# V's second last half in two transfers of 1 MB, and half of its P.V ahead of the merge of head 14

## The chip, the cores and the metric

The kernel runs on one core of one Trainium2 chip. Times are device microseconds (us) of one execution. A shorter time is better. The engines are named as in the profile: PE (matrix multiply), PEld (its weight loads), DVE (vector), ACT (activation), POOL, and SP, whose queue issues the large transfers. "Granted clock" is the share of its full clock that the chip lets PE have. All executions quoted were fast, that is, none was more than 1.5% above the fastest of its kernel.

## The reference

One query row attends to 8192 keys, in each of 16 heads of width 256, in bf16.

```
B, H, Sq, Sk, D = 1, 16, 1, 8192, 256
# q: [B,H,Sq,D], k and v: [B,H,Sk,D], all bf16
scores = einsum("bhqd,bhkd->bhqk", q, k) * D ** -0.5
p = softmax(scores, axis=-1)
return einsum("bhqk,bhkd->bhqd", p, v)
```

K and V together are 134.2 MB, and each of their elements is used once. The kernel can't take less time than their transfer.

## The kernel before

Each head's K and each head's V come in two halves of 2 MB. A half has 32 columns, and a column is a 128x256 piece of bf16. The halves are numbered 0 to 31, so head 14 has 28 and 29, and head 15 has 30 and 31. The first half of K and the last half of V already came in pieces:

```python
HALF = 32
V_SLOTS = 2 * UNROLL          # 4 buffers for halves of V
FIRST_CUT = (4, 4, 8, 16)
LAST_CUT = (16, 8, 4, 4)
# ...
        def cuts(kind, n):
            if kind == "k" and n == 0:
                return FIRST_CUT
            if kind == "v" and n == NIT - 1:
                return LAST_CUT
            return (HALF,)
```

All K and V transfers are issued in a fixed order on SP's queue. Each piece has a semaphore, and a transfer waits only until its buffer is free:

```python
        for kind, h, x in items:
            # ... n: number of the half, slot = n % slots
            if n >= slots:
                waits = [f"{kind}free{n - slots}"] + ([f"ktfree{n - slots}"] if kind == "k" else [])
            cs = cuts(kind, n)
            at = 0
            for i, wd in enumerate(cs):
                if kind == "k":
                    s = sem_l[slot] if i == 0 else s_first[i - 1]
                else:
                    s = sem_l[slot] if i == len(cs) - 1 else s_last[i]
                used[id(s)] = used.get(id(s), 0) + 16
                plan.op("sp", ..., f"{kind}{n}.{i}", waits, dma=(s, used[id(s)]))   # (cut)
                at += wd
```

P.V of a half, `pv`, multiplies the softmax weights (`E`) with the columns of V and adds up in the accumulator `acc`. It runs on PE and waits column by column for the piece that holds the column. Head 15 takes one column of V at a time, the other heads take two. For those, `merge` adds the two partial rows that this leaves, with weights from DVE:

```python
        def pv(n, c0=0, c1=HALF):
            # ... head h, buffer slot, accumulator a
            step = 1 if h == H - 1 else 2
            for c in range(c0, c1, step):
                pe(lambda e, c=c, col=col: e.matmul(
                        a[0:step, 0 : step * D],
                        lhsT=E[:, col : col + step],
                        rhs=Vb[slot][:, c * D : (c + step) * D],
                        start=(x == 0 and c == 0), stop=(x == 1 and c == HALF - step)),
                    f"vfree{n}" if c == HALF - step else None,
                    [f"e{h}", first_free] + landed("v", n, c, c + step))

        def merge(h):
            act(...)                 # copies acc[s][0:2, :] to ac[s], waits for vfree{2*h+1}
            for i in range(2):
                pe(...)              # acc[s][0:1, 0:D] += w2[:, i].T @ ac[s][:, i*D:(i+1)*D]
```

This is the end of the program on PE, after its loop over the heads. The loop's last pass ends with P.V of half 27 and the merge of head 13.

```python
        n = 2 * (H - 2)
        pv(n)                            # half 28
        softmax(H - 1)
        pv(n + 1, 0, HALF // 2)          # half 29
        softmax2(H - 1)
        pv(n + 1, HALF // 2, HALF)
        lmm(H - 1)                       # row sums of head 15
        n += 2
        pv(n, 0, HALF // 4)              # half 30: 8 columns
        merge(H - 2)
        final(H - 2)
        # ... output of heads 0 to 14, from ACT's queue
        pv(n, HALF // 4, HALF)           # half 30: 24 columns
        pv(n + 1)                        # half 31
        final(H - 1)
        # ... output of head 15
```

## Time and profile before

| | before |
|---|---|
| median of the first three runs, us | 327.12 (326.97 to 327.27) |
| profiled execution, us | 327.36, span 325.6 |
| landings of V's half 29, half 30 and the last piece of half 31, us | 310.27, 315.18, 320.15 |
| PE's last matmul ends, us | 323.51 |

From the page of the kernel before: busy time by engine, then lines of the forty slices of the span. A digit is tenths of a slice of 8.14 us, PEclk is the granted clock in tenths.

```profile
PE 238.7 (73%) x1746; PEld 112.4 (35%) x1746; DVE 281.4 (86%) x1624; ACT 100.8 (31%) x200; POOL 0.2 (0%) x4
...
PEclk9999999969899898979598989779689877898999
DMA  7999999999999999999999999999999999999990
...
q1 hardware_dynamic: 10080, 134.22, 97.4%
```

The DMA engines are busy for 90% or more of all slices except the first and the last, and queue q1, with K and V, keeps them busy for 97.4% of the span. This kernel waits for bytes. A change that moves no bytes can gain only at the end, where the bytes have come and work is left.

The timeline of PE in that end, kernel before. The columns are start, us from the first start to the last end, engine and line, operation, output and inputs, count. In brackets stand the idle time just ahead and what ended it. L610 is P.V, L632 the merge, L589 the row sums.

```profile
300.51 3.62 PE L610 MATMUL acc<-Vb,E 128*2 128x512 bf16 x16 [0.84 <-DMA Vb<-in_v_dram]
304.80 1.02 PE L632 MATMUL acc<-ac,w 2*1 2x256 f32 x4 [0.68 <-ACT ac L625]
305.75 3.61 PE L610 MATMUL acc<-Vb,E 128*2 128x512 bf16 x16
...
310.31 1.89 PE L610 MATMUL acc<-Vb,E 128*2 128x512 bf16 x8 [0.73 <-DMA Vb<-in_v_dram]
...
314.16 0.19 PE L589 MATMUL misc<-ones_col,lsum 128*2 128x1 f32 x2
315.32 1.03 PE L610 MATMUL acc<-Vb,E 128*1 128x256 bf16 x8 [0.96 <-DMA Vb<-in_v_dram]
316.28 1.02 PE L632 MATMUL acc<-ac,w 2*1 2x256 f32 x4
317.23 6.27 PE L610 MATMUL acc<-Vb,E 128*1 128x256 bf16 x56
```

The first three lines are P.V of half 27, the merge of head 13, and P.V of half 28. PE waits 0.73 us for half 29 and 0.96 us for half 30, and after 315.32 it waits for nothing. At that time half 31 is still arriving, but always ahead of PE.

The chain of waits of the same kernel, at its end, in order of time (start, length, what). Here and below, pieces of it named "issue", of 0.14 us or less, are left out.

```profile
296.77 18.41 DMA Vb<-in_v_dram
315.32 1.03 PE acc L610 x8
316.35 0.95 PE acc L632 x4
317.30 6.22 PE acc L610 x56
323.54 0.47 ACT o L654
```

The transfer in this chain is half 30, issued at 296.77 when P.V of half 26 freed its buffer. From its landing on, everything is work of PE and then one copy on ACT.

### The profile page before, as it was taken

What the parts mean: (1) busy time and instruction counts of PE and PEld (TensorE: products, weight loads), DVE (VectorE), ACT (ScalarE), POOL (GpSimd) and SP (SyncE); (2) the same over time, 40 slices, a digit from 0 to 9 for tenths busy, and PEclk for the clock granted to TensorE, in tenths of its full rate; (3) what the DMA queues carried; (4) which work ended last, traced back from release to release, by engine and by line L of the source; (5) the groups of instructions that cost most, each with busy time, mean ns of one, the idle gap of its engine ahead of it and who ended that gap; (6) DMA issues with size and microseconds to landing.
All of it is one profiled execution on the core that took longest, in us unless ns stands there. A gap on an engine that the chain in (4) does not pass through costs nothing.

```text
span 325.6 us, 5646 instructions
## 1 busy us (share of the span) xinstructions
PE 238.7 (73%) x1746; PEld 112.4 (35%) x1746; DVE 281.4 (86%) x1624; ACT 100.8 (31%) x200; POOL 0.2 (0%) x4
## 2 busy tenths in 40 slices
PE   1554328788787868787878866887786788777977
PEld 0333223343333333333334333332333324333335
DVE  3799999999999999999999998888988888988400
ACT  2362321332424242333133242222324213242110
POOL 0000000000000000000000000000000000000000
PEclk9999999969899898979598989779689877898999
DMA  7999999999999999999999999999999999999990
GB/s 256 426 437 425 426 429 425 431 429 425 428 433 427 425 431 433 421 431 431 427 427 431 429 425 433 431 421 432 433 423 427 428 433 423 431 431 425 431 387 19
DMA packets 10126, 134.35 MB, mean 413 GB/s; under 512 B 1138, under 2 KB 1155, under 8 KB 1924
## 3 DMA queue, kind: packets, MB, share of 16 engines
q1 hardware_dynamic: 10080, 134.22, 97.4%
q8 instruction: 4, 0.07, 0.1%
q14 instruction: 6, 0.05, 0.0%
q10 hardware_dynamic: 36, 0.02, 0.0%
HBM read 134.23 MB, written 0.01 MB: 412 GB/s over the span
## 4 chain that ended last, share of the span: by engine, by line
DVE 52%; DMA 34%; PE 6%; issue 5%; ACT 1%; DVEq 1%; SPq 0%
DVE prod L362 48%; DMA Kb<-in_k_dram 18%; DMA Vb<-in_v_dram 16%; PE acc L610 5%; DVE S L362 2%; DVE w L341 1%; PE acc L632 1%; DVE g L331 1%; ACT KT L504 0%; DVE colf L285 0%; DVE recip L339 0%; DVEq L144 0%; ACT ac L625 0%; DVE m L381 0%; PE tp L495 0%
## 5 line engine op out<-in xcount | busy, mean ns | idle before, releaser
L362 DVE CUSTOM_DVE_ANT_0 prod<-Kb,qbc 128x256 bf16<-128x256 bf16 x768 | 269.3, 411 | 21.5 <-DMA Kb<-in_k_dram 12.5
L610 PE MATMUL acc<-Vb,E 128*2 128x512 bf16 (+1 forms) x544 | 148.2, 437 | 7.1 <-DMA Vb<-in_v_dram 7.0
L504 ACT ACTIVATE KT<-tp 128x1024 bf16<-128x1024 bf16 x64 | 62.0, 1021 | 115.1 <-PE tp L495 115.1
L610 PEld LDWEIGHTS acc<-Vb,E 128*2 128x2 bf16 (+1 forms) x544 | 49.8, 95 | 91.6 <-issue 49.0
L362 DVE DVE_READ_ACCUMULATOR2_ANT S<- 128x1 f32 x768 | 56.7, 74 | 0.0
L495 PE MATMUL tp<-identb,Kb 128*128 128x128 bf16 x512 | 38.2, 234 | 5.0 <-DMA Kb<-in_k_dram 5.0
L521 PE MATMUL spe<-qcur,KT 128*128 128x1 bf16 x512 | 21.6, 165 | 23.3 <-ACT KT L504 23.2
L495 PEld LDWEIGHTS tp<-identb,Kb 128*128 128x128 bf16 x512 | 32.3, 105 | 15.8 <-issue 14.9
L521 PEld LDWEIGHTS spe<-qcur,KT 128*128 128x128 bf16 x512 | 16.8, 98 | 28.9 <-ACT KT L504 28.7
L625 ACT ACTIVATE ac<-acc 2x512 f32<-2x512 f32 x15 | 8.8, 587 | 58.0 <-PE acc L610 58.0
L632 PE MATMUL acc<-ac,w 2*1 2x256 f32 x60 | 15.3, 373 | 9.5 <-ACT ac L625 9.5
L560 PE MATMUL misc<-g,ones_row 1*128 1x1 f32 x32 | 6.8, 280 | 17.3 <-DVE g L331 17.3
L549 PE MATMUL misc<-ident,m 128*1 128x128 f32 x34 | 7.1, 293 | 14.7 <-DVE m L381 14.7
L560 PEld LDWEIGHTS misc<-g,ones_row 1*128 1x128 f32 x32 | 5.5, 213 | 20.4 <-DVE g L331 19.9
L647 ACT ACTIVATE o<-acc 1x256 bf16<-1x256 f32 x15 | 5.6, 373 | 17.9 <-PE acc L632 17.9
L632 PEld LDWEIGHTS acc<-ac,w 2*1 2x1 f32 x60 | 3.5, 77 | 20.9 <-ACT ac L625 16.6
L549 PEld LDWEIGHTS misc<-ident,m 128*1 128x1 f32 x34 | 1.5, 81 | 21.5 <-DVE m L381 15.3
L331 DVE TENSOR_REDUCE g<-misc 1x1 f32<-1x128 f32 x17 | 4.7, 274 | 5.0 <-PE misc L549 5.0
L567 ACT ACTIVATE negb<-misc 128x1 f32<-128x1 f32 x16 | 2.8, 174 | 13.6 <-PE misc L560 13.6
L339 DVE RECIPROCAL recip<-misc 2x1 f32<-2x1 f32 x17 | 2.6, 151 | 4.5 <-PE misc L589 4.5
L589 PE MATMUL misc<-ones_col,lsum 128*2 128x1 f32 x34 | 3.2, 164 | 3.9 <-ACT E L574 3.1
L574 ACT ACTIVATE E<-S,negb 128x64 bf16<-128x64 f32 x16 | 5.6, 348 | 0.5
(34 smaller groups left out, 39.6 us busy)
## 6 DMA issues: line engine op xcount, KB each, us to landing
Kb<-in_k_dram SPq DMA_DIRECT2D x31, 2048.0 KB, 23.4
Vb<-in_v_dram SPq DMA_DIRECT2D x31, 2048.0 KB, 28.2
Kb<-in_k_dram SPq DMA_DIRECT2D x1, 1024.0 KB, 7.8
Vb<-in_v_dram SPq DMA_DIRECT2D x1, 1024.0 KB, 13.5
Kb<-in_k_dram SPq DMA_DIRECT2D x2, 256.0 KB, 3.0
Kb<-in_k_dram SPq DMA_DIRECT2D x1, 512.0 KB, 4.5
Vb<-in_v_dram SPq DMA_DIRECT2D x1, 512.0 KB, 14.3
Vb<-in_v_dram SPq DMA_DIRECT2D x2, 256.0 KB, 14.6
```

The costliest lines, as they stand in the source:

```text
L331: lambda e: e.tensor_reduce(g[0:1, s : s + 1], misc[s][0:1, MT0 : MT0 + P], AX.X, ALU.max),
L362: lambda e, slot=slot, c=c, col=col, h=h, r=(ttr - 1) % PROD: e.tensor_tensor_reduce(out=prod[:, r * D : (r + 1) * D], in0=Kb[slot][:, c * ...
L495: lambda e, c=c, hf=hf, i=(b * NH + hf) * P, view=view: e.transpose(view[:, i : i + P], Kb[slot][:, c * D + hf * P : c * D + (hf + 1) * P] ...
L504: lambda e, gn=gn, view=view: e.activation(out=KT[gn % KT_SLOTS][:, :], in_=view[:, 0 : GROUP * D], func=ACT.Copy),
L521: lambda e, b=b, hf=hf, oc=oc, gn=gn: e.matmul(spe[sl(h)][:, oc : oc + 1], lhsT=KT[gn % KT_SLOTS][:, (b * NH + hf) * P : (b * NH + hf + 1) ...
L549: lambda e: e.matmul(misc[s][0:1, MT0 : MT0 + P], lhsT=m[:, s : s + 1], rhs=ident[:, :], start=True, stop=True),
L560: lambda e: e.matmul(misc[s][:, BC0 : BC0 + 1], lhsT=ones_row[0:1, :], rhs=g[0:1, s : s + 1], start=True, stop=True),
L574: lambda e: e.activation(out=E[:, s * J : (s + 1) * J], in_=S[:, s * J : (s + 1) * J], func=ACT.Exp, bias=negb[:, h : h + 1], scale=SCALE, ...
L610: lambda e, c=c, col=col: e.matmul(a[0:step, 0 : step * D], lhsT=E[:, col : col + step], rhs=Vb[slot][:, c * D : (c + step) * D], start=(x ...
L625: lambda e: e.activation(out=ac[s][:, :], in_=acc[s][0:2, :], func=ACT.Copy),
L632: lambda e, i=i: e.matmul(acc[s][0:1, 0:D], lhsT=w2[0:2, 2 * s + i : 2 * s + i + 1], rhs=ac[s][0:2, i * D : (i + 1) * D], start=(i == 0), ...
L647: lambda e: e.activation(out=o[0:1, h * D : (h + 1) * D], in_=acc[s][0:1, 0:D], func=ACT.Copy),
```

## The change

The intent: the columns of half 30 that PE needs first should not wait for the columns that it needs last. The half comes in two transfers of 1 MB, and the whole of the first is used before the merge of head 14.

```diff
+BEFORE_CUT = (16, 16)
...
-        s_last = [sem(f"s_l{i}") for i in range(len(LAST_CUT) - 1)]
+        s_last = [sem(f"s_l{i}") for i in range(len(LAST_CUT) + len(BEFORE_CUT) - 2)]
...
                 return LAST_CUT
+            if kind == "v" and n == NIT - 2:
+                return BEFORE_CUT
             return (HALF,)
...
-                    s = sem_l[slot] if i == len(cs) - 1 else s_last[i]
+                    s = sem_l[slot] if i == len(cs) - 1 else s_last[i + (len(LAST_CUT) - 1) * (n == NIT - 2)]
...
-        pv(n, 0, HALF // 4)
+        pv(n, 0, HALF // 2)
         merge(H - 2)
         final(H - 2)
...
-        pv(n, HALF // 4, HALF)
+        pv(n, HALF // 2, HALF)
         pv(n + 1)
```

## The prediction

> **What bounds the kernel.** The transfers. The page gives the DMA engines 97% of the span at 413 GB/s; the forty slices show them full until about 317 us of 325.6. PE is busy 73%, DVE 86%. Only the tail can gain from this change: everything before waits for bytes whose number and order stay.
>
> **The tail, from the timeline of PE and the landings in the trace.** V's last halves land 4.9 us apart: number 29 at 310.27, 30 (the changed one) at 315.18, and 31, already in four pieces, at 317.67, 318.88, 319.51 and 320.15 us. PE starts P.V of 29 at 310.31 and works without a gap until the row-sum matmul of head 15 ends at 314.35. Then it is idle 0.96 us, released by the DMA of Vb at 315.32 (the chain of waits goes through that 18.41 us transfer too). From there PE never idles: 8 columns of head 15, merge of head 14 (first matmul 316.28), 56 columns from 317.23 to 323.50. A column costs (323.50 - 317.23)/56 = 0.112 us, the merge holds PE 0.95 us. A copy on ACT (0.47) and the output's DMA end the run. The last V byte lands 3.3 us before PE ends, so this stretch is PE-bound.
>
> **What the change does.**
> 1. Half 30 comes as two transfers of 1 MB, in order on one queue, so the first should be complete half of 4.91 us before the second: 315.18 - 2.45 = 312.7 us (an estimate from these landings). PE is free only at 314.35: its 0.96 us wait goes whole, with 1.6 us to spare. The Trainium skill ("DMA: Bandwidth & Descriptors", Why a DMA increments its semaphore by 16) says that only the full 16 means that all has landed; the trace agrees: for half 30, fifteen increments are in by 313.86, the last at 315.18. I put the same lag into the 312.7.
> 2. Sixteen instead of eight columns before the merge: 8 x 0.112 = 0.9 us moves ahead of it, nothing is added. The merge's inputs are ready either way: the ACT copy ends at 314.95, DVE's weights at 314.81; eight columns from 314.35 would end at about 315.25. I expect the move alone to be worth about 0.
> 3. One more issue on SP's queue, 0.33 to 0.43 us, after that at 296.77; the next issue waits until 304.16 for a buffer, so it is hidden. Half 31 took 4.97 us in four pieces against 4.91 in one: cutting should cost under 0.1 us, against over 1 us of slack.
>
> **New tail.** PE starts head 15 at 314.35: 16 columns to 316.15, merge to 317.1, 48 columns to 322.5. Needs: second half of 30 at 317.1 (landed 315.2); 31's pieces at 318.9, 320.7, 321.6, 322.0 (landed 317.7, 318.9, 319.5, 320.2). No new wait. Gain 0.96 to 1.0 us, all on the critical path.
>
> **Predicted time** 327.12 - 0.97 = 326.15 us, range 325.8 to 326.55. Faster by over 2%: 0.01; within 2%: 0.98; slower: 0.01.
>
> **Right or wrong in the profile.** The 0.96 us idle before head 15's first columns is gone; the first 1 MB lands near 312.7; merge begins near 316.1; PE ends near 322.5, with no wait on 31's pieces; the last landing stays near 320.2; before 310 us nothing differs.
>
> **What would make it wrong.** The first piece landing after 314.35; smaller pieces delaying half 31 by over 1 us; a half-clock window (3.4 us, granted 0.5 elsewhere in the trace; the tail from 295.9 us had 1.0) falling on the tail, costing up to 1.7 us.

## The result, and the profile after

| | before | after |
|---|---|---|
| median, us (six runs each) | 327.28 (326.97 to 328.11) | 326.19 (325.47 to 327.01) |
| profiled execution, us | 327.36, span 325.6 | 326.87, span 325.1 |
| V's landings: 29, first of 30, all of 30, all of 31, us | 310.27, none, 315.18, 320.15 | 310.09, 312.58, 315.06, 320.07 |
| PE's last matmul ends, us | 323.51 | 323.03 |

The ratio is 0.9965, with a 95% interval of 0.9944 to 0.9985. A ratio here is the mean time of one kernel's fast runs over that of the other's in the same rounds, so it isn't quite the ratio of the medians. The change is a gain clear of noise, about 1.1 us by the medians, and within 2%.

The lines of the page after that answer to those of before:

```profile
PE 237.1 (73%) x1746; PEld 112.2 (35%) x1746; DVE 281.3 (87%) x1624; ACT 101.0 (31%) x200; POOL 0.2 (0%) x4
...
PEclk9999999979898996979797989877898697798799
DMA  7999999999999999999999999999999999999991
...
q1 hardware_dynamic: 10224, 134.22, 97.6%
```

The queue has 144 packets more: 128 rows are cut in two, and there are 16 more semaphore increments. The bytes and the load of the engines are the same. One thing differs that the change doesn't touch: in PEclk, the third digit from the end (the slice from 300.7 to 308.8 us) is a 7, and it was a 9 before. The trace's clock records have a window of 3.41 us at half clock from 301.49 us, and before has no such window after 295.88.

The timeline of PE in the tail, kernel after. The line numbers have moved by three (P.V is now L613, the merge L635).

```profile
300.34 5.30 PE L613 MATMUL acc<-Vb,E 128*2 128x512 bf16 x16 [0.85 <-DMA Vb<-in_v_dram]
306.32 1.02 PE L635 MATMUL acc<-ac,w 2*1 2x256 f32 x4 [0.68 <-ACT ac L628]
307.27 3.61 PE L613 MATMUL acc<-Vb,E 128*2 128x512 bf16 x16
...
310.94 1.89 PE L613 MATMUL acc<-Vb,E 128*2 128x512 bf16 x8
...
314.79 0.19 PE L592 MATMUL misc<-ones_col,lsum 128*2 128x1 f32 x2
314.84 1.91 PE L613 MATMUL acc<-Vb,E 128*1 128x256 bf16 x16
316.68 1.02 PE L635 MATMUL acc<-ac,w 2*1 2x256 f32 x4
317.63 5.40 PE L613 MATMUL acc<-Vb,E 128*1 128x256 bf16 x48
```

The wait for half 30 is gone, as intended. The wait for half 29 is gone too, which the change can't have done. P.V of half 27 took 5.30 us instead of 3.62, because the half-clock window fell on it, so PE came to half 29 late. That is why this pair of profiles differs by 0.5 us where the medians differ by 1.1.

The end of the chain of waits, kernel after:

```profile
265.49 34.81 DMA Vb<-in_v_dram
300.34 5.32 PE acc L613 x16
305.68 0.60 ACT ac L628
306.32 1.02 PE acc L635 x4
307.34 3.54 PE acc L613 x16
...
317.70 5.35 PE acc L613 x48
```

Before, the last transfer in the chain was half 30, and PE's share began at 315. After, the last transfer is half 27, and the chain stays on PE (with one copy on ACT) from 300 us on. This is the second effect of the change: the tail is no longer held by a transfer near its end, so it now depends on how fast PE ran in the 15 us before.

### A reading without the start's noise

Executions differ by up to 1.1 us in when V lands, whatever the kernel. I therefore measured each profiled execution's tail from its own landings. The last column is the time of that execution minus V's last landing, and the window is any half-clock window starting between 295 and 315 us.

| kernel (profiled execution) | half-clock window | head 15 starts after half 29 landed, us | PE ends after V's last landing, us | time minus V's last landing, us |
|---|---|---|---|---|
| before | none | 5.05 | 3.35 | 7.21 |
| after | 301.49 | 4.75 | 2.96 | 6.80 |
| after, second time | 300.50 | 4.71 | 2.94 | 6.79 |
| split only | none | 3.95 | 2.18 | 6.07 |
| order only | 300.72 | 5.06 | 3.34 | 7.20 |
| pieces swapped | none | 5.11 | 3.36 | 7.21 |
| after + added matmuls | none | 3.95 | 2.19 | 6.07 |
| the same, PE made late | none | 4.69 | 2.94 | 6.79 |
| before + added matmuls | none | 5.04 | 3.33 | 7.18 |
| the same, PE made late | none | 5.06 | 3.36 | 7.25 |
| after, half 29 cut too | none | 2.98 | 1.22 | 5.08 |
| the same + added matmuls | none | 3.00 | 1.22 | 5.09 |
| after, halves 28 and 29 cut too | none | 2.60 | 1.19 | 5.07 |
| the same + added matmuls | none | 2.62 | 1.18 | 5.03 |

The five profiles in which half 30's first columns don't land early show 7.18 to 7.25 us, whatever else happened. With the first columns early it is 6.07 us when PE is on time, and 6.8 us when PE is late. So the change is worth about 1.14 us (7.21 - 6.07) in the first case and 0.41 us (7.21 - 6.80) in the second. The last four lines belong to the experiments that cut further halves, below.

### The profile page after: what moved, and what is told of

It is laid out like the page before. It is cut to its first block, busy times and chain, and to the rows that moved or that the text cites. A ratio compares the mean times of both kernels' runs of the same rounds, so it can differ in the third digit from the quotient of the medians.

```text
span 325.1 us, 5647 instructions
## 1 busy us (share of the span) xinstructions
PE 237.1 (73%) x1746; PEld 112.2 (35%) x1746; DVE 281.3 (87%) x1624; ACT 101.0 (31%) x200; POOL 0.2 (0%) x4
## 4 chain that ended last, share of the span: by engine, by line
DVE 57%; DMA 29%; PE 7%; issue 5%; DVEq 1%; ACT 0%; SPq 0%
DVE prod L365 52%; DMA Kb<-in_k_dram 19%; DMA Vb<-in_v_dram 11%; PE acc L613 6%; DVE S L365 2%; DVE w L344 1%; PE acc L635 1%; DVE g L334 1%; DVE colf L288 0%; DVE recip L342 0%; DVEq L145 0%; DVE m L384 0%; ACT ac L628 0%; ACT o L657 0%; DVEq L138 0%
## 5 line engine op out<-in xcount | busy, mean ns | idle before, releaser
L613 PE MATMUL acc<-Vb,E 128*2 128x512 bf16 (+1 forms) x544 | 147.2, 436 | 6.0 <-DMA Vb<-in_v_dram 6.0
L613 PEld LDWEIGHTS acc<-Vb,E 128*2 128x2 bf16 (+1 forms) x544 | 49.8, 95 | 89.4 <-issue 46.6
L635 PE MATMUL acc<-ac,w 2*1 2x256 f32 x60 | 15.3, 373 | 9.5 <-ACT ac L628 9.5
L635 PEld LDWEIGHTS acc<-ac,w 2*1 2x1 f32 x60 | 3.5, 77 | 20.9 <-ACT ac L628 16.6
```

What stands on the lines that cost most here:

```text
L613: lambda e, c=c, col=col: e.matmul(a[0:step, 0 : step * D], lhsT=E[:, col : col + step], rhs=Vb[slot][:, c * D : (c + step) * D], start=(x ...
L635: lambda e, i=i: e.matmul(acc[s][0:1, 0:D], lhsT=w2[0:2, 2 * s + i : 2 * s + i + 1], rhs=ac[s][0:2, i * D : (i + 1) * D], start=(i == 0), ...
```

## The experiments

My theory ("landing"): the gain is the 0.96 us wait for half 30, taken away because the first 1 MB lands earlier, and nothing else. The rivals: "order" (the eight more columns ahead of the merge do it), "two issues" (the second issue, its semaphore or its shorter packets do it), and "phase" (it is only chance of the half-clock windows).

The first four kernels shared one chip and eleven runs of the kernel before (median 327.06; three of the eleven, at 328.6 to 328.8, pull the ratios down a little and widen the intervals so much that they overlap). The four can be compared directly, though: their means are 326.21 (the change again) and 326.30 us (split only) against 327.16 (order only) and 326.89 (pieces swapped).

### The changed kernel again (after_again)

No edit.

> The changed kernel, timed again on this chip beside the three others. Theory (landing): the 0.96 us wait of PE before head 15's columns is gone because the first 1 MB lands about 2.5 us before the second; ratio to before 0.9965 to 0.9975 (0.8 to 1.1 us less). Second part of the theory, about the spread: the tail of this kernel is bound by PE from about 305 us on, so its time moves with where the half-clock windows (granted 0.5 for 3.4 us) fall: executions with one between 300 and 312 us end about 0.5 to 1.5 us later than those without. Rival (phase only): the gain is chance of those windows, and the ratio here is 1.000 within 0.001.

Measured: 326.15 us (325.41 to 327.04, six runs), ratio 0.9962 (0.9937 to 0.9987). The gain repeats, which speaks against phase alone. Its profiled execution again had a half-clock window, from 300.50 us, and again P.V of half 27 took 5.27 us. The spread of 1.6 us is also there again.

### The split alone (split_only)

```diff
 # against the changed kernel
-        pv(n, 0, HALF // 2)
+        pv(n, 0, HALF // 4)
         merge(H - 2)
...
-        pv(n, HALF // 2, HALF)
+        pv(n, HALF // 4, HALF)
```

> Two transfers of 1 MB, but only eight columns before the merge, as before the change. Theory (landing): all of the gain, ratio equal to that of the changed kernel within 0.001; in the profile no wait for V before head 15's first column. Rival (order): the gain comes from putting eight more columns ahead of the merge of head 14, whose inputs are late; then this ratio is 1.000, and the profile shows PE waiting for ACT's copy before the merge.

Measured: 326.40 us (325.68 to 326.93, six runs), ratio 0.9968 (0.9942 to 0.9993). The timeline of PE, this kernel:

```profile
310.63 1.89 PE L613 MATMUL acc<-Vb,E 128*2 128x512 bf16 x8 [0.72 <-DMA Vb<-in_v_dram]
...
314.48 0.19 PE L592 MATMUL misc<-ones_col,lsum 128*2 128x1 f32 x2
314.53 1.03 PE L613 MATMUL acc<-Vb,E 128*1 128x256 bf16 x8
315.50 1.02 PE L635 MATMUL acc<-ac,w 2*1 2x256 f32 x4
316.44 6.27 PE L613 MATMUL acc<-Vb,E 128*1 128x256 bf16 x56
```

This execution had no half-clock window in the tail, so the wait of 0.72 us for half 29 is as before, and the effect of the split can be read alone. Head 15 starts 0.05 us after the row sums, with no wait for V, and no wait stands before the merge after eight columns. PE ends 2.18 us after V's last landing, against 3.35 before. All of the gain is in the split: the one profile of the change's own order without a late PE, that of the run with added matmuls below, ends 2.19 us after the landing, which is the same.

### The order alone (order_only)

```diff
 # against the kernel before
-        pv(n, 0, HALF // 4)
+        pv(n, 0, HALF // 2)
         merge(H - 2)
...
-        pv(n, HALF // 4, HALF)
+        pv(n, HALF // 2, HALF)
```

> One transfer of 2 MB as before, sixteen columns before the merge. Theory (landing): ratio 1.000 within 0.001; if PE is ready for head 15 at time t, it waits until the 2 MB have landed at about 315.2 us, whatever the order after that. Rival (order): ratio 0.997, as the changed kernel.

Measured: 327.15 us (326.93 to 327.60, six runs), ratio 0.9993 (0.9970 to 1.0016). No gain. The timeline of PE, this kernel:

```profile
300.75 5.27 PE L610 MATMUL acc<-Vb,E 128*2 128x512 bf16 x16 [1.71 <-DMA Vb<-in_v_dram]
...
315.16 0.19 PE L589 MATMUL misc<-ones_col,lsum 128*2 128x1 f32 x2
315.55 1.91 PE L610 MATMUL acc<-Vb,E 128*1 128x256 bf16 x16 [0.20 <-DMA Vb<-in_v_dram]
```

This execution did have a half-clock window (300.72 us), and it cost nothing. PE reached the row sums 0.78 us later than in the kernel before, counted from half 29's landing (4.67 against 3.89 us), but half 30 had still not landed (315.42), so the wait shrank to 0.20 us and head 15 started 5.06 us after half 29 landed, against 5.05 before. The rival "order" falls.

### The pieces the other way round (swapped)

```diff
 # against the changed kernel
-            at = 0
-            for i, wd in enumerate(cs):
+            pieces = [(i, sum(cs[:i]), wd) for i, wd in enumerate(cs)]
+            if kind == "v" and n == NIT - 2:
+                pieces.reverse()
+            for i, at, wd in pieces:
```

> Two transfers of 1 MB with the same semaphores and the same order of columns on PE as the changed kernel, but the half that PE needs second is issued first. Theory (landing): the first sixteen columns then land about 315.2 us, so the wait is back and the ratio is 1.000 within 0.001. Rival (two issues or two semaphores by themselves, for example shorter packets): ratio 0.997, as the changed kernel.

Measured: 326.90 us (326.61 to 327.10, six runs), ratio 0.9989 (0.9966 to 1.0012). The timeline of PE, this kernel:

```profile
313.36 0.19 PE L593 MATMUL misc<-ones_col,lsum 128*2 128x1 f32 x2
314.57 1.91 PE L614 MATMUL acc<-Vb,E 128*1 128x256 bf16 x16 [1.02 <-DMA Vb<-in_v_dram]
```

Two issues, two semaphores and 8 KB rows are all there, and PE's order is that of the changed kernel. Only the columns that PE needs first come second (they landed at 314.44 here, in an execution in which V's last halves all landed 0.7 to 0.8 us earlier than in the profile of before). The wait is back whole, and so is the 7.21 us from V's last landing to the end. The timed ratio, 0.9989, is just outside the 1.000 within 0.001 that I expected, but its interval holds 1. The rival "two issues" falls. What counts is when the first columns land.

### The spread: more work on PE (warm)

The changed kernel's six timed executions spread over 1.5 and 1.6 us, those of the two kernels without the early landing over 0.7 and 0.5 us. The kernel before is no clear witness here: its runs spread over 1.1 us in the first six, and over 2.1, 0.9 and 0.6 us in the three later sets of eleven. So that the change widens the spread is not shown by the timed runs. To see if half-clock windows make the spread, I gave PE more to do, in the hope that the clock would stay up. The results of these matmuls are read by nobody; the kernel's outputs stay correct.

```diff
 # against the changed kernel (shortened)
+        def warm(h, times):
+            for _ in range(times if h >= 2 else 0):
+                pe(lambda e: e.matmul(misc[sl(h)][:, 256:512], lhsT=identb[:, :],
+                                      rhs=qb[:, 0:256], start=True, stop=True),
+                   None, [f"qb{H - 1}"])
...
         def k_score(n):
             for gi in range(NG):
                 gn = n * NG + gi
+                warm(h, 5 if gi == 0 else 4)
```

> The changed kernel plus nine matmuls of 128x256 per half of a head (from head 2 on) whose result nobody reads, put where PE waits for ACT. Theory (phase): the changed kernel's spread (1.3 to 1.6 us over six executions, against 0.3 to 0.5 us where PE waits for half 30) comes from whether a half-clock window falls on the P.V of half 27; six executions of the changed kernel differ so. If more work on PE keeps the granted clock at 1.0, every execution should look like the good ones: median about 325.5 to 325.9, spread under 0.7 us, mean clock over 0.95, PE's wait for half 29 back at about 0.7 us. Rival: the spread comes from elsewhere (start-up, DMA); then it stays over 1.2 us with the clock at 1.0. If the clock stays at 0.9, the run decides nothing on this, and is likely slower by up to 1 us.

The next four kernels shared one chip and eleven runs of the kernel before (median 327.06). Measured: 325.86 us (325.58 to 326.15, five runs), ratio 0.9958 (0.9945 to 0.9971). The median and the spread came as the theory said, but not by the way it said: the mean granted clock was 0.905 to 0.921, hardly more than the 0.90 without, and the wait for half 29 was 0.16 us, not 0.7:

```profile
310.16 1.89 PE L624 MATMUL acc<-Vb,E 128*2 128x512 bf16 x8 [0.16 <-DMA Vb<-in_v_dram]
```

By its own words the run decides nothing about the clock, and the loss of up to 1 us that I expected in this case didn't come. What can be said is weaker. Of the eight profiles without the added matmuls three had a half-clock window between 295 and 315 us, of the six with them none. The added work may have moved the windows away; fourteen profiles don't prove it.

### Half 29 cut as well (cut29), and with the added matmuls (warm_cut29)

```diff
-            if kind == "v" and n == NIT - 2:
+            if kind == "v" and NIT - 3 <= n < NIT - 1:
                 return BEFORE_CUT
 # and one semaphore more
```

> Half 29 cut in two as well. Theory: in executions without a half-clock window near 301 us PE waits 0.72 us for half 29, and that wait goes, up to 0.7 us less; in executions with such a window PE comes later than half 29 lands, and nothing changes. Median 0 to 0.7 us below the changed kernel's (325.5 to 326.2, ratio 0.994 to 0.9965). PE ends 11.4 to 12.9 us after half 29 has landed, against 12.1 (no window) and 12.9 (window) in the changed kernel's form.

> The two together. Theory: if the added matmuls keep the clock at 1.0, half 29's wait of 0.7 us is there in every execution and the cut takes it in every execution: median 0.6 to 0.9 us below the run with the added matmuls alone, spread under 0.7 us. If the clock is still 0.9, the difference between the two is between 0 and 0.5 us.

Measured for the cut alone: 326.60 us (324.60 to 326.94, six runs), ratio 0.9972 (0.9950 to 0.9994). The median missed what I expected (325.5 to 326.2): two executions were at 324.60 and 324.95, the other four at 326.48 to 326.94. The profiled one is the one at 324.95. It had no half-clock window in the tail, PE did not wait for half 29, and it ended 1.22 us after V's last landing, 0.96 us better than the split alone. I expected 0.7. From the softmax matmul before half 29 to P.V of half 29 it is 1.10 us with the wait (309.53 to 310.63) and 0.22 us without (308.78 to 309.00), so here the wait cost more than the 0.72 us of idle time that its line shows. The lines without the wait:

```profile
308.78 0.38 PE L552 MATMUL misc<-ident,m 128*1 128x128 f32 x2
309.00 1.89 PE L613 MATMUL acc<-Vb,E 128*2 128x512 bf16 x8
```

The four slow ones fit the case of a late PE, but they have no trace, so this is argued, not shown. The mean granted clock of every execution fits too: 0.905 in the two fast ones, 0.895 to 0.900 in the four slow ones, and one window of 3.41 us at half clock is 0.005 of this mean. It doesn't tell where in the execution the windows were.

Measured with the added matmuls: 324.92 us (324.66 to 325.68, six runs), ratio 0.9933 (0.9920 to 0.9945). That is 0.94 us below the run with the added matmuls alone. This expectation was missed: I had tied 0.6 to 0.9 us to a clock of 1.0 and said 0 to 0.5 us if the clock was still about 0.9. The clock was 0.91 to 0.926, and yet the gain was over both. The wait doesn't explain all of it. In the profile with the added matmuls alone, P.V of half 29 began 0.55 us after the softmax matmul started, and 0.22 us after it in this one, so the cut itself took about 0.33 us; the rest is that PE came to half 27 later in the former (0.61 us after half 27 landed, against 0.04). Whether that lateness is chance or comes of the cut isn't shown. The spread, 1.02 us, is over the 0.7 that I expected, but none of the six executions is near 326.5.

### Halves 28, 29 and 30 cut, half 28 ahead of the merge of head 13 (cut28), and with the added matmuls (warm_cut28)

```diff
-            if kind == "v" and n == NIT - 2:
+            if kind == "v" and NIT - 4 <= n < NIT - 1:
                 return BEFORE_CUT
...
             if h >= 2:
                 pv(2 * (h - 2) + 1)
+                if h == H - 1:
+                    pv(2 * (H - 2), 0, HALF // 2)
                 merge(h - 2)
...
-        plan.mark("pe")      # the last pass of PE's loop is now written out
         n = 2 * (H - 2)
-        pv(n)
+        pv(n, HALF // 2, HALF)
```

> Halves 28, 29 and 30 cut in two, and the first sixteen columns of half 28 put before the merge of head 13 (the last pass of PE's loop is written out for that). Theory: PE's 0.7 us wait for ACT's copy before that merge is filled, and with it the loss of a half-clock window near 301 us is made up in part; PE ends 11.0 to 12.3 us after half 29 has landed, median 325.0 to 325.8 (ratio 0.992 to 0.9955). If PE's end is instead set by V's last landing (about 320.2 us), a rest of 0.1 us of work and 0.5 us of ACT bounds the gain at about 2 us below the changed kernel.

> The best form that the runs point to: halves 28, 29 and 30 cut in two, half 28's first columns ahead of the merge of head 13, and the unread matmuls. Theory: faster than both kernels, ratio 0.990 to 0.993, median 324.2 to 325.0; PE ends 1.2 to 1.9 us after V's last landing, with waits for pieces of V back in the tail, that is near the bound of the transfers.

Measured for the first: 325.46 us (324.57 to 326.55, six runs), ratio 0.9948 (0.9930 to 0.9966), as expected. The timeline of PE, this kernel:

```profile
312.91 1.91 PE L613 MATMUL acc<-Vb,E 128*1 128x256 bf16 x16 [0.29 <-DMA Vb<-in_v_dram]
314.75 1.02 PE L635 MATMUL acc<-ac,w 2*1 2x256 f32 x4
315.70 1.91 PE L613 MATMUL acc<-Vb,E 128*1 128x256 bf16 x16
317.80 3.65 PE L613 MATMUL acc<-Vb,E 128*1 128x256 bf16 x32 [0.19 <-DMA Vb<-in_v_dram]
```

PE is ahead of the bytes again: it waits for the first piece of half 30 (landed at 312.78) and for the first of half 31 (landed at 317.75). From there 32 columns are left, 3.65 us, which outlast the last landing at 320.27. That is why this kernel's tail (1.19 us) is hardly shorter than that of the cut of half 29 alone (1.22). The next thing to cut would be the first 1 MB of half 31; I didn't try it.

With the added matmuls, in the last four runs with their own eleven runs of before (median 326.93): 324.92 us (324.82 to 325.24, five runs), ratio 0.9941 (0.9928 to 0.9954). The median is in the range that I expected, the ratio isn't (0.990 to 0.993). It beats the kernel before by 2.0 us on the same chip. Against the changed kernel, which was timed in other sets of runs, it is 1.2 to 1.3 us by the medians and 0.7 to 0.8 by the ratios. It has the smallest spread of those that beat both, but it is no better than the cut of half 29 with the added matmuls.

### How much slack PE has: warm_before, warm_before_late, warm_late

Here I doubled the suspected cause of the spread by hand: PE is made late by a fixed amount, planned as 0.96 us (an estimate; nine at the 0.109 us between two of them in the trace of warm are 0.98) and measured as 1.09 (from the merge of head 13 to P.V of half 28 it was 2.04 us instead of 0.95), in the kernel before and in the changed one. All have the added matmuls. The "late" ones have nine more ahead of P.V of half 28.

```diff
 # warm_before is the kernel before with the edit of "warm"; then, for the late ones
         n = 2 * (H - 2)
+        warm(H - 1, 9)
         pv(n)
```

> The kernel before with the nine unread matmuls of 128x256 per half of a head. Theory (landing): its end is set by the 2 MB of half 30, which land about 315.2 us whatever PE did earlier; the added work makes PE neither the first nor the last to be waited for, so the ratio is 1.000 within 0.001 and the wait before head 15's first column is 0.8 to 1.2 us. Rival: the added matmuls by themselves make any of these kernels faster; then 0.999 or less, as much as the changed kernel gained by them (0.3 us).

> As the run of the kernel before with added matmuls, with nine more of 128x256 [...]on PE ahead of the P.V of half 28. Theory: PE has 0.7 to 1.7 us of waits after that point, for halves 29 and 30, so the added 0.96 us shortens waits and does not show: median within 0.3 us of the same kernel without them. Rival (PE already bounds the tail of the kernel before, and the gain is only less PE idle): 0.8 to 1.0 us slower.

> The changed kernel with the added matmuls, and the same nine more on PE ahead of the P.V of half 28. Theory: after that point PE waits only 0.16 to 0.7 us for half 29 and then never, so the added 0.96 us comes through but for that wait: median 0.3 to 0.8 us above the run without the nine more (325.86), and no wait for V from half 29 on. Rival (the transfers still bound the changed kernel's tail): no change.

Measured, in the same last four runs:

| | median, us | ratio to before (95%) |
|---|---|---|
| warm_before | 326.98 (326.86 to 327.57, five runs) | 1.0008 (0.9995 to 1.0021) |
| warm_before_late | 327.65 (326.88 to 327.78, five runs) | 1.0020 (1.0007 to 1.0033) |
| warm_late | 326.64 (325.71 to 327.77, six runs) | 0.9993 (0.9976 to 1.0011) |

The added matmuls by themselves gain nothing in the kernel before, as expected. The changed kernel got slower by the late work: by the medians 0.78 us (326.64 against 325.86, on two chips), within what I expected, and by the ratios 0.0035, or 1.1 us, which is more. The timelines of PE, first the kernel before with PE late, then the changed one:

```profile
310.28 1.89 PE L621 MATMUL acc<-Vb,E 128*2 128x512 bf16 x8
...
315.00 1.03 PE L621 MATMUL acc<-Vb,E 128*1 128x256 bf16 x8 [0.68 <-DMA Vb<-in_v_dram]
```

```profile
310.74 1.89 PE L624 MATMUL acc<-Vb,E 128*2 128x512 bf16 x8
...
314.59 0.19 PE L603 MATMUL misc<-ones_col,lsum 128*2 128x1 f32 x2
314.64 1.91 PE L624 MATMUL acc<-Vb,E 128*1 128x256 bf16 x16
```

In the first the work took up the wait for half 29 and part of the wait for half 30, and there are 0.68 us left, so the tail has the length it had: 3.36 us after V's last landing, against 3.33. In the second there is no wait left that could take it up, and the tail grew from 2.19 to 2.94 us, which are the figures of an execution with a half-clock window. So a PE that comes about a microsecond late is enough to explain the longer tail in these profiles.

One expectation was missed. By the median, warm_before_late is 0.67 us slower than warm_before, where I said at most 0.3. Its profiled execution, at 327.07 us, isn't slower; three of the other four, at about 327.7, are. They have no trace. A half-clock window on top of the late work would use up the slack, but that isn't shown. So the timed runs support the cushion less than the profiles do: the late work cost 0.67 us in the kernel before and 0.78 in the changed one by the medians, about 0.4 and 1.1 by the ratios.

## Why the prediction was right

- **The size.** I predicted 326.15 us and the median was 326.19. The sum held: the wait of 0.96 us before head 15 is the step that went, and in the undisturbed pair of profiles (before, and the split alone) head 15 started 1.10 us earlier, counted from the landing of half 29 (5.05 to 3.95). The 0.13 us beyond my 0.97 came from the term "PE is free only at 314.35". I took that from the recorded end of the row-sum matmul. The next matmul starts 0.05 us after that one starts, not after it ends. The Trainium skill ("Perfetto Trace Analysis", Tensor Engine Instruction) says that the reported end of a matmul is computed, not observed. The trace agrees that such an end is not when the next may start: 314.48 plus 0.19 is 314.67, and the next began at 314.53.
- **The landing.** I estimated 312.7 us for the first 1 MB, and it was 312.58. V's last landing stayed at 320.07 (predicted 320.2). No wait on half 31's pieces appeared.
- **The order.** I said that the move of eight columns was worth about 0. Alone it gave 0.9993, and with the split but without the move the gain was there.
- **What was wrong.** "Before 310 us nothing differs" failed in the profile: a half-clock window at 301.49 made P.V of half 27 take 5.30 instead of 3.62 us. So the merge of head 14 began at 316.68, not near 316.1, and PE ended at 323.03, not near 322.5. I had named such a window as a risk, of up to 1.7 us. I hadn't seen that the change itself makes the kernel open to it. Before, the waits for halves 29 and 30 (0.73 and 0.96 us) hid a late PE. After, only the first is left. My range of 325.8 to 326.55 held the median but only two of the six executions. That the median came within 0.04 us of my number is luck: the interval of the ratio reaches from about 0.5 to 1.8 us, and the profiled pair differs by 0.5. What was right is the mechanism, and the size of the wait.

The half-clock windows are the clock gate of the Trainium skill ("TensorE: Matmul & The Clock Gate", Part 1): half rate, decided in windows of about 3.4 us that run free of the kernel's start. The traces agree on all three: granted 0.5, 3.413 us long or twice that, and at other times in each execution (292.47, 291.25, 290.26 and 292.26 us in four of them). Within one execution all windows start on one grid of 3.413 us, to the nanosecond or two, and this grid stands differently against the kernel each time. The kernel before and "order only" are the same program until the eight moved columns, after 315 us, yet the second met a window at 300.72 us and the first none; so it is the execution that decides, and not the change. In the eight traces without added matmuls the place of the grid sorts the cases: where a window came, a point of the grid lay between 0.03 us before and 1.15 us after the start of P.V of half 27 (three traces); where none came, the nearest lay at least 0.65 us before or 1.52 after it (five). Eight traces don't make this a rule.

What stays open: what the gate goes by when it closes between 295 and 315 us, how many of the executions without a trace had such a window, and so whether the windows make the whole of the 1.5 us spread. V's landing times differ by up to 1.1 us between profiles (319.40 to 320.54), and that enters the spread too. Most of this is how late the last of a transfer's 16 semaphore increments comes: in these two executions the first increment of V's last piece came at 316.45 and 316.71 us, only 0.26 apart.

## What to carry to other kernels

When a kernel is bound by transfers, look at the last wait of the engine that ends it, and cut the transfer there so that what is needed first lands first; here the columns' landing did everything and the order of the work around it nothing. A wait that you take away was also a cushion: afterwards the time depends on everything upstream that used to end within the wait, so the spread may grow (the profiles show a tail of 6.07 or 6.8 us; the timed runs here are too noisy to show it), and measure the tail from a landing instead of from the start. And once one wait is gone the next one up the chain is worth the same look: in the profiles, cutting one half more was worth another microsecond when PE was on time, cutting a third one almost nothing. Without the added matmuls the median of the first of these cuts, 326.60 us, was no better than that of the change.

## What the Trainium skill lacked or had wrong

- "TensorE: Matmul & The Clock Gate" (HAM oscillation) gives as its abstract rule that PE must have no idle gap over about 3.4 us. Taken as enough to keep full clock, it fails here. In the trace of before, between 60 and 320 us, PE's longest gap in the records is 2.20 us, and still there are 16 stretches at half clock, 64.9 us together. More work on PE (nine matmuls of 128x256 per half of a head) didn't end this either: the mean granted clock went from 0.90 to between 0.905 and 0.921.
- "DMA: Bandwidth & Descriptors" (Why a DMA increments its semaphore by 16) says that the engines finish on their own and only the full 16 counts. It gives no figure for how far apart they are in a full queue: for half 30 before, the first increment came at 311.60 us, the fifteenth at 313.86 and the sixteenth at 315.18. The last step, 1.32 us here, is the execution's own (0.38 us for the same bytes in the profile after); the spread from first to last was 3.0 to 4.0 us for half 30 in all fourteen profiles. When a piece of 1 MB was cut off, its increments spread over 2.99 us (309.59 to 312.58), those of the second MB in the same execution over as much (312.07 to 315.06), and those of half 29, still one transfer of 2 MB, over 2.98: a smaller piece didn't make the last engine less late.
- No page that I read says that a wait that is taken away makes the time depend more on the clock gate's phase: 7.20 us from V's last landing to the end with a half-clock window and 7.21 without, in kernels with the wait, against 6.80 with and 6.07 without, in kernels that have lost it.
